# Moves of small steps to GpSimd, exits of v's products in one copy, no comparison for empty rows, and a fifth pair in four-step products

## The chip, the cores and the metric

The kernel runs on one core of a Trainium2 chip. The metric is the device time of one execution in microseconds. Three runs of the kernel before took 1397.51, 1401.68 and 1403.38 us; their median, 1401.68 us, is the time before. The core has five engines that work side by side, each in the order of its own instructions: TensorE (PE; its weight loads are listed as PEld), VectorE (DVE), ScalarE (ACT), GpSimd (POOL) and the queue that issues transfers (SP). They wait for each other by semaphores.

## The reference

Attention of 8 batches with 8 heads over 576 tokens with 64 features, in which a score counts only if it is within tau of its row's maximum, and then two layers of an MLP (4608 tokens, 512 to 2048 to 512) with a leaky step between them:

```python
scores = scale * np.matmul(q, k.transpose(0, 1, 3, 2))
thresh = np.max(scores, axis=-1, keepdims=True) - tau
scores = np.where(scores >= thresh, scores, -1000000000.0)
scores = scores - np.max(scores, axis=-1, keepdims=True)
attn = np.exp(scores)
attn = attn / (np.sum(attn, axis=-1, keepdims=True) + 1e-09)
x = np.matmul(attn, v)            # then heads side by side: 4608 x 512
h = x @ w_in
g = np.maximum(h, 0.0) + alpha * np.minimum(h, 0.0)
out = (g @ w_out).astype(np.float32)
```

The weights w_in and w_out arrive as float64 and are read as pairs of 32-bit words; the kernel makes two float32 parts (high and low) of each.

## The kernel before

**Pairs, units, cycles.** Two heads of one batch make a pair; there are 32. A pair has nine units of 128 rows of queries (`UNITS`): four chunks for each head and one tail that holds the last 64 rows of both. The program runs in cycles, one unit per cycle, nine cycles a pair, from cycle -3 to 291. In cycle i the mask of unit i is applied, the scores of unit i + 2 are computed, and maximum and exp of unit i + 2 follow (before cycle `SW` = 52 these come in twos: in an odd cycle i the maximum and exp of unit i + 1 at its start and of unit i + 2 at its end). The chain of a unit is: `scores` on TensorE into one of two PSUM buffers `s` (L395); `rowmax` on DVE, the negated maximum `nmx` (L410); `expo` on ACT, `p` (L418), and then the threshold `thr` = maximum - tau (L423, ACT); `mask` on DVE (L430), which compares the scores with `thr`, multiplies `p` and sums the row into `sm`, and with which the buffer `s` is free again; `turn` on TensorE (L439, L455), which transposes `p`.

**Whole and split pairs.** The transposed `p` is copied out of PSUM for the product with v. In the first `WHOLE` = 4 pairs it is copied whole, as float32 (L499, three copies in four on ACT and one on DVE), and the product (L542, `avmul`) runs in TensorE's slower float32 form with 64 columns of v, one matmul per block. In the other 28 pairs it is split into a high part (`hi`, L491, ACT) and a low part (`lo`, L495, DVE), v likewise (`prep_vh` L370 on ACT, `prep_vl` L375 on POOL), with high and low part of v as 64 + 64 columns of one operand `vst`; two matmuls per block. The product of a split pair leaves PSUM in `avout` in two copies on ACT, of 64 partitions each: the high half into `xa` (L553) and the low half into `xb` (L555).

**The end of a pair.** `recip` adds 1e-9 to the sums and inverts them (L560, L561, DVE); `rturn` and `rout` bring the result by way of DRAM into `rb`, spread over 64 partitions; `fin_add` (POOL) adds `xb` to `xa` for a split pair (L582, L586) and takes the mean of v into `vs` (L583); `fin_mul` multiplies with `rb` (L589, POOL); `fin_un` (L592, DVE) compares `rb` with 1e8 to find rows that kept no score and puts `vs` there; `fin_out` adds that (L595, POOL) and writes `xs` (L596, SP). The cycles for these, counted from the pair's first, are in `FINW` (whole) and `FINS` (split).

**Beside it.** q and k of later pairs are loaded, split and doubled ten or more cycles ahead: `prep_kl` (L332) and `prep_ql` (L357) on POOL, the scaling of q by 0.125 on ACT (L345 into `qst`, L350 in place), and moves between partitions on SP (L337 to L364). Seven pieces of w_in and seven of w_out are decoded in cycles -3 to 40, a new piece every three cycles (`Split64`): `size` on ACT, `clamp` (L127), `shift` (L130), `sign` (L135) and `power` (L140) on DVE, `round` on ACT, `rest` (L148, L149) and `join` (L152) on POOL. Which of DVE and POOL takes clamp and the two products of `rest` is in `ENG1`, letters v and p. From cycle 49 on `Mlp` puts layer 1 and 2 for 7 of the 16 blocks of w_in beside attention (`pha`, `acca`, `ga`); how much goes into a cycle is planned by counts, not by time. What is left follows in `drain`, with the decoding of the other weights, and then the other nine blocks (`phb`, `accb`).

**What sets the order.** On PE, ACT, DVE and POOL the instructions stand in the order in which the program names them, cycle by cycle; `at_cycle` puts a step into a cycle. The order in SP's queue is set by a scheduler. An engine that waits holds up everything behind it.

## Time and profile before

| | |
|---|---|
| median of three runs | 1401.68 us |
| span of the profiled execution | 1397.3 us |
| busy TensorE, DVE, ACT, POOL | 1339.4, 975.7, 820.9, 762.3 us |
| instructions on DVE, ACT, POOL | 1933, 1843, 821 |
| bytes moved by DMA | 157.67 MB, 113 GB/s in the mean |
| granted clock of TensorE | 0.9 or more of full speed in every one of 40 slices |

Attention takes the first 823 us or so (the last mask stands at 820.80 us), the drain goes on to about 950 us, and the rest is the second part of the MLP. A row of a table of stages reads: start and end of the stage, its length, and for each engine the busy time and, in brackets, the number of instructions; then the granted clock, the share of time in which the DMA engines were busy, and GB/s. A row of groups reads: line, engine, operation, tiles written and read, shapes, count; busy time in us and the mean of one in ns; idle time of the engine just before them and who ended it. A row of a timeline: start and duration in us, engine, line, operation. A row of waits: who waited for whom, us in total, times, the longest.

### The profile page before, as it was taken

How to read it: one execution, taken by the hardware profiler on the slowest of the kernel's cores; microseconds unless marked ns; L12 is line 12 of the kernel's file. 1: busy time of each engine (PE TensorE's matmuls, PEld its weight loads, DVE VectorE, ACT ScalarE, POOL GpSimd, SP SyncE). 2: the span in 40 equal slices, each digit the busy share in tenths (PEclk: the TensorE clock that was granted, in tenths of full speed). 3: DMA queues.
4: the chain of work that ended last, by engine and by line, in shares of the span. 5: the costliest groups of instructions: out<-in, count | busy, mean ns of one | idle time of the engine just before them, and what ended most of it. 6: DMA issues, size and time to landing. Idle time of an engine off the chain costs nothing.

```text
span 1397.3 us, 23301 instructions
## 1 busy us (share of the span) xinstructions
PE 1339.4 (96%) x8116; PEld 1181.2 (85%) x8116; DVE 975.7 (70%) x1933; ACT 820.9 (59%) x1843; POOL 762.3 (55%) x821
## 2 busy tenths in 40 slices
PE   5888899999999999999999999888999999999998
PEld 4556789999999999999999998777888888888887
DVE  6999988888888898898888957986323323323332
ACT  7788888888888888888888854453112012111100
POOL 3776676666676666576676557566434124223311
PEclk9999999999999999999999999999999999999999
DMA  8643634545545444454454214433320220111011
GB/s 249 184 127 106 180 105 122 162 116 142 147 117 150 139 134 131 132 154 127 128 160 132 83 57 153 132 109 128 121 74 17 91 91 33 59 61 42 19 61 38
DMA packets 94628, 157.67 MB, mean 113 GB/s; under 512 B 14160, under 2 KB 39024, under 8 KB 94512
## 3 DMA queue, kind: packets, MB, share of 16 engines
q1 hardware_dynamic: 94512, 156.19, 38.4%
q8 instruction: 65, 1.06, 0.3%
q14 instruction: 51, 0.42, 0.1%
HBM read 85.53 MB, written 28.46 MB: 82 GB/s over the span
## 4 chain that ended last, share of the span: by engine, by line
PE 80%; DVE 9%; ACT 4%; DMA 2%; issue 2%; POOL 2%; SPq 0%; DVEq 0%; POOLq 0%; ACTq 0%
PE phb L194 16%; PE accb L224 16%; PE s L395 10%; PE av L542 10%; PE acca L224 9%; PE pha L194 9%; PE t L439 7%; DVE p L430 2%; DVE nmx L410 2%; DMA wri<-in_moe_w_in_dram 1%; PE tk L455 1%; DVE wti L135 1%; POOL wi L152 1%; ACT xb L555 1%; ACT xa L553 1%
## 5 line engine op out<-in xcount | busy, mean ns | idle before, releaser
L410 DVE TENSOR_REDUCE nmx<-s 128x1 f32<-128x576 f32 x288 | 217.0, 753 | 72.6 <-PE s L395 69.5
L215 ACT ACTIVATE gb<-ptb 128x512 fp32r<-128x512 f32 x81 | 50.9, 630 | 337.7 <-DVE ptb L873 337.3
L218 POOL TENSOR_TENSOR gb<-ptb,gb 128x512 fp32r<-128x512 f32 x81 | 104.4, 1290 | 257.0 <-ACT gb L215 256.8
L224 PE MATMUL acca<-wo,ga 128*128 128x512 f32 x756 | 230.7, 419 | 7.2 <-ACT ga L215 4.0
L224 PE MATMUL accb<-wo,gb 128*128 128x512 f32 x972 | 221.9, 389 | 0.0
L224 PEld LDWEIGHTS accb<-wo,gb 128*128 128x128 f32 x972 | 182.4, 188 | 37.9
L430 DVE SCALAR_TENSOR_TENSOR p<-s,thr,p 128x576 f32<-128x576 f32 x256 | 206.6, 807 | 1.3 <-ACT thr L423 0.9
L194 PE MATMUL phb<-xh,wi 128*128 128x512 f32 x648 | 202.9, 392 | 1.1 <-ACT xh L180 1.1
L194 PE MATMUL pha<-xh,wi 128*128 128x256 f32 x1008 | 199.7, 284 | 3.7 <-DVE pta L873 3.4
L418 ACT ACTIVATE p<-s,nmx 128x576 f32<-128x576 f32 x256 | 190.0, 742 | 10.8 <-DVE nmx L410 10.5
L395 PE MATMUL s<-kh,qst 128*128 128x288 f32 x640 | 142.2, 312 | 38.1 <-DVE p L430 23.3
L194 PEld LDWEIGHTS pha<-xh,wi 128*128 128x128 f32 x1008 | 163.8, 190 | 9.9 <-DVE pta L873 4.6
L224 PEld LDWEIGHTS acca<-wo,ga 128*128 128x128 f32 x756 | 132.8, 191 | 28.6 <-ACT ga L215 5.3
L439 PE MATMUL t<-ident,p 128*128 128x128 f32 x1024 | 154.6, 274 | 0.0
L395 PEld LDWEIGHTS s<-kh,qst 128*128 128x128 f32 x640 | 101.4, 193 | 61.5 <-issue 29.4
L903 DVE TENSOR_TENSOR ob<-accb,pin 128x512 f32<-128x512 f32 x36 | 24.2, 689 | 181.9 <-PE accb L224 181.9
L194 PEld LDWEIGHTS phb<-xh,wi 128*128 128x128 f32 x648 | 122.6, 189 | 27.2 <-ACT xh L180 1.5
L194 PE MATMUL pha<-xl,wi 128*128 128x256 f32 x504 | 142.2, 282 | 0.0
L872 DVE TENSOR_SCALAR ptb<-phb,alpha_sb 128x512 f32<-128x512 f32 x81 | 60.7, 751 | 108.5 <-PE phb L194 96.4
L395 PE MATMUL s<-kl,qst 128*128 128x288 f32 x640 | 133.8, 299 | 0.0
L194 PE MATMUL phb<-xl,wi 128*128 128x512 f32 x324 | 127.2, 393 | 3.6 <-POOL xl L182 3.6
L439 PEld LDWEIGHTS t<-ident,p 128*128 128x128 f32 x1024 | 126.5, 141 | 0.1
(117 smaller groups left out, 2772.6 us busy)
## 6 DMA issues: line engine op xcount, KB each, us to landing
kr<-in_k_dram SPq DMA_DIRECT2D x31, 320.0 KB
rb<-rvd SPq DMA_DIRECT2D x64, 144.0 KB
...
```

The source lines that it names most:

```text
L194: nc.tensor.matmul(ph[:, :n], w[:, c, :], xx[:, c, :n], start=(c == 0 and ti == 0), stop=(c == NCC - 1 and ti == 2),)
L215: nc.scalar.activation(g[:, 0, :n], t[:, :n], AF.Copy)
L218: nc.gpsimd.tensor_tensor(g[:, 1, :n], t[:, :n], f(g[:, 0, :n]), op=ALU.subtract)
L224: nc.tensor.matmul(acc[:m, :], gg[:, g, o : o + m], w, start=(first and ti == 0), stop=(last and ti == 2))
L395: nc.tensor.matmul(ps[:, h, :288], w, kk[:, a + h * 288 : a + (h + 1) * 288], start=(ki == 0 and i == 0), stop=(ki == 1 and i == n - 1),)
L410: nc.vector.tensor_reduce(self.nmx[:, j : j + 1], self.S[u][0][:, :, :288], axis=AX.XY, op=ALU.max, negate=True)
L418: nc.scalar.activation(pj, ps[:, :, :288], AF.Exp, bias=nmx[:, j : j + 1], scale=1.0)
L430: nc.vector.scalar_tensor_tensor(pj, ps[:, :, :288], thr[:, j : j + 1], pj, op0=ALU.is_ge, op1=ALU.mult, accum_out=self.sm[:, c : c + 1])
L439: nc.tensor.transpose(tb[:, c, :], pt[:, j, j * D + c * P : j * D + (c + 1) * P], ident)
L542: nc.tensor.matmul(pa[:m, :n], w, x, start=(part == 0 and c == 0), stop=(part == z.parts[-1] and c == NKC))
L872: nc.vector.tensor_scalar(t[:, :n], ph[:, :n], 0.0, alpha_sb[:, fc : fc + 1], op0=ALU.min, op1=ALU.mult)
L903: nc.vector.tensor_tensor(ob[:m], acc[:m], pi_[:m], op=ALU.add)
```

## The change

- `clamp` of all 14 early pieces goes from DVE to POOL (`ENG1`), with minimum and maximum in the other order; `shift` comes a cycle later, just ahead of `sign`.
- The threshold of units before cycle 50 (`THRP`) is computed on POOL instead of ACT. The scaling of q in place (L350) goes from ACT to POOL, the addition before the reciprocal from DVE to POOL.
- A fifth pair, pair 4, is whole (`WHOLE`); the memory of the whole pairs and the decoding is given to the MLP in cycle 49 instead of 41 (`SPC`).
- For split pairs the second head's v has its low part in the first 64 columns and its high part in the others. `avout` copies all 128 partitions at once, of the first head into `xa` and of the second into `xb`. Three moves in SP's queue (`part_low`, `part_high`) bring the low parts together in `xl` (in the buffer of `qt`) and the high parts in `xa`. `prep_vl` becomes two instructions.
- The comparison for empty rows goes. `vs` is now 1e-9 times the mean of v and is added to the sum ahead of the multiplication with `rb`, by POOL, with one input tensor; the addition in `fin_out` goes.
- `FINW` and `FINS` move the last steps: `xs` of a split pair is written in cycle 18 of the pair instead of 16, of a whole pair in 17 as before.

```diff
-ENG1 = ('vpp', 'vpp')
+ENG1 = ('ppp', 'ppp')
-THR = 'a'
+THRP = 50
-FINW = (9, 10, 11, 14, 16, 16, 17)
-FINS = (9, 11, 12, 12, 15, 16, 16)
+FINW = (9, 10, 11, 14, 14, 15, 16)
+FINS = (9, 11, 12, 13, 14, 16, 17)
-SPC = 41
-WHOLE = 4
+SPC = 49
+WHOLE = 5
...
-            self.eng[0].tensor_scalar(f(self.t), f(self.t), WORD_LO, WORD_HI, op0=ALU.max, op1=ALU.min)
+            self.eng[0].tensor_scalar(f(self.t), f(self.t), WORD_HI, WORD_LO, op0=ALU.min, op1=ALU.max)
...
-            nc.scalar.activation(self.qr, self.qr, AF.Copy, scale=0.125)
+            nc.gpsimd.tensor_scalar(self.qr, self.qr, 0.125, None, op0=ALU.mult)
...
-            self.vst = ap1.tile([P, 10, P], F32R, tag="vst", name=f"vst{self.pi}", bufs=2)
-            nc.scalar.activation(self.vst[:, :, :D], self.vr, AF.Copy)
+            self.vst = ap1.tile([P, 11, P], F32R, tag="vst", name=f"vst{self.pi}", bufs=2)
+            at = self.vst.rearrange("p c d -> p (c d)").rearrange("p (j r) -> p j r", j=2)
+            self.vh = at[:, :, : 5 * P].rearrange("p j (c d) -> p j c d", d=P)[:, :, :, :D]
+            nc.scalar.activation(self.vh, self.vr.rearrange("p (j c) d -> p j c d", j=2), AF.Copy)
...
-            nc.gpsimd.tensor_tensor(self.vst[:, :, D:], self.vr, f(self.vst[:, :, :D]), op=ALU.subtract)
+            for j in range(2):
+                vl = self.vst[:, 5 * j : 5 * j + 5, (1 - j) * D : (2 - j) * D]
+                nc.gpsimd.tensor_tensor(vl, self.vr[:, 5 * j : 5 * j + 5], f(self.vh[:, j]), op=ALU.subtract)
...
-            if THR == "p" and 9 * self.pi + u >= SW:
+            if 9 * self.pi + u < THRP:
                 nc.gpsimd.tensor_scalar(self.S[u][2][:, c], nmx[:, c], -1.0, tau_sb, op0=ALU.mult, op1=ALU.subtract)
...
-            r, cs = slice(j * D, (j + 1) * D), slice(col, col + n)
-            nc.scalar.activation(self.xa[r, cs], pa[:D, :n], AF.Copy)
-            if not self.whole:
-                nc.scalar.activation(self.xb[r, cs], pa[D:, :n], AF.Copy)
+            if self.whole:
+                nc.scalar.activation(self.xa[j * D : (j + 1) * D, cs], pa[:D, :n], AF.Copy)
+            else:
+                nc.scalar.activation((self.xb if j else self.xa)[:, cs], pa[:, :n], AF.Copy)
+        def part_low(self):
+            if not self.whole:
+                self.xl = ap1.tile([P, S + 4], F32, tag="qt", name=f"xl{self.pi}", bufs=1)
+                nc.sync.dma_start(self.xl[:D, 2:], self.xa[D:, 2:])
+                nc.sync.dma_start(self.xl[D:, : S + 2], self.xb[:D, : S + 2])
+        def part_high(self):
+            if not self.whole:
+                nc.sync.dma_start(self.xa[D:, : S + 2], self.xb[D:, : S + 2])
...
-            nc.vector.tensor_scalar(self.rv, self.sm, 1e-9, None, op0=ALU.add)
+            nc.gpsimd.tensor_scalar(self.rv, self.sm, 1e-9, None, op0=ALU.add)
             nc.vector.reciprocal(self.rv, self.rv)
...
-                nc.gpsimd.tensor_scalar(self.vs[r], xa[r, cs], 1.0 / S, None, op0=ALU.mult)
+                nc.gpsimd.tensor_scalar(self.vs[r], xa[r, cs], 1e-9 / S, None, op0=ALU.mult)
...
+        def fin_un(self):
+            nc.gpsimd.tensor_scalar(self.x, self.x, self.vs, None, op0=ALU.add)
         def fin_mul(self):
             nc.gpsimd.tensor_tensor(self.x, self.x, self.rb, op=ALU.mult)
-        def fin_un(self):
-            nc.vector.tensor_scalar(self.rb, self.rb, 1e8, self.vs, op0=ALU.is_ge, op1=ALU.mult)
         def fin_out(self):
-            nc.gpsimd.tensor_tensor(self.x, self.x, self.rb, op=ALU.add)
             nc.sync.dma_start(xs[self.b][self.hp], self.x)
...
-        at_cycle(o + fin[3], p.fin_add)
-        at_cycle(o + fin[4], p.fin_mul)
+        at_cycle(o + fin[3], p.part_low)
+        at_cycle(o + fin[4], p.part_high)
+        at_cycle(o + fin[5], p.fin_add)
         at_cycle(o + fin[5], p.fin_un)
-        at_cycle(o + fin[6], p.fin_out)
+        at_cycle(o + fin[6], p.fin_mul)
+        at_cycle(o + fin[6] + 1, p.fin_out)
...
-        at_cycle(c + 2, w.shift)
+        at_cycle(c + 3, w.shift)
```

Three places in the order of the instructions follow. In a row stand the line, the operation, the tile written and the tiles read, and the size; the lines of the changed kernel are its own (L426 is the threshold, L579 the addition before the reciprocal, L609 `fin_un`, L612 the product with `rb`).

POOL in cycles 24 to 26, near the end of pair 2 (`vs`, `xa` or `x` and `rb` belong to pair 1, `kl` to pair 3, `wro`, `wto`, `wo` to pieces of w_out). Before:

```order
L583 TENSOR_SCALAR vs_963<-xa_729 64x1 x2
L148 TENSOR_TENSOR wro_746<-wro_746 128x512
L149 TENSOR_TENSOR wto_845<-wto_845,wo_973 128x512
L589 TENSOR_TENSOR xa_729<-xa_729,rb_878 128x576
L332 TENSOR_TENSOR kl_1028<-kr_970,kh_1026 128x640
L152 TENSOR_TENSOR wo_973<-wto_845,wro_746 128x512
L595 TENSOR_TENSOR xa_729<-xa_729,rb_878 128x576
```

After:

```order
L603 TENSOR_SCALAR vs_992<-x_729 64x1 x2
L609 TENSOR_SCALAR x_729<-x_729,vs_992 128x576
L148 TENSOR_TENSOR wro_746<-wro_746 128x512
L149 TENSOR_TENSOR wto_844<-wto_844,wo_969 128x512
L426 TENSOR_SCALAR thr_7_973<-nmx_7_972,tau_sb 128x1
L612 TENSOR_TENSOR x_729<-x_729,rb_877 128x576
L332 TENSOR_TENSOR kl_1026<-kr_966,kh_1024 128x640
L152 TENSOR_TENSOR wo_969<-wto_844,wro_746 128x512
L426 TENSOR_SCALAR thr_0_1038<-nmx_0_1037,tau_sb 128x1
L127 TENSOR_SCALAR wto_1031<-wto_1031 128x512
L426 TENSOR_SCALAR thr_0_1038<-nmx_0_1037,tau_sb 128x1
```

The steps that were there stand in the same order; thresholds now stand between them, a clamp stands at the end, and the last addition (L595) has become `fin_un` (L609) ahead of the product.

DVE in cycles 25 to 27, where pair 3 begins (`s_7`, `s_8` are the last units of pair 2, `s_0`, `s_1` the first of pair 3). Before:

```order
L430 SCALAR_TENSOR_TENSOR p_3_979,sm_715<-s_7_950,thr_7_977,p_3_979 128x576
L410 TENSOR_REDUCE nmx_7_976<-s_8_983 128x1
L592 TENSOR_SCALAR rb_878<-rb_878,vs_963 128x576
L135 SCALAR_TENSOR_TENSOR wto_940<-wro_848,wto_940 128x512
L410 TENSOR_REDUCE nmx_0_1038<-s_0_1005 128x1
L430 SCALAR_TENSOR_TENSOR p_3_979,sm_715<-s_8_983,thr_7_977,p_3_979 128x576
L140 TENSOR_SCALAR wro_848<-wto_940 128x512
L127 TENSOR_SCALAR wto_1032<-wto_1032 128x512
L430 SCALAR_TENSOR_TENSOR p_0_1041,sm_1004<-s_0_1005,thr_0_1039,p_0_1041 128x576
L410 TENSOR_REDUCE nmx_0_1038<-s_1_1045 128x1
L560 TENSOR_SCALAR rv_1092<-sm_715 128x9
L561 RECIPROCAL rv_1092<-rv_1092 128x9
```

After:

```order
L435 SCALAR_TENSOR_TENSOR p_3_975,sm_716<-s_7_949,thr_7_973,p_3_975 128x576
L415 TENSOR_REDUCE nmx_7_972<-s_8_979 128x1
L130 TENSOR_SCALAR wto_939<-wto_939 128x512
L135 SCALAR_TENSOR_TENSOR wto_939<-wro_847,wto_939 128x512
L415 TENSOR_REDUCE nmx_0_1037<-s_0_1004 128x1
L435 SCALAR_TENSOR_TENSOR p_3_975,sm_716<-s_8_979,thr_7_973,p_3_975 128x576
L140 TENSOR_SCALAR wro_847<-wto_939 128x512
L435 SCALAR_TENSOR_TENSOR p_0_1040,sm_1003<-s_0_1004,thr_0_1038,p_0_1040 128x576
L415 TENSOR_REDUCE nmx_0_1037<-s_1_1044 128x1
L580 RECIPROCAL rv_1090<-rv_1090 128x9
```

Comparison (L592), clamp (L127) and addition (L560) are gone; shift (L130) and sign (L135) stand side by side, and the reciprocal, alone, reads what POOL's L579 writes.

SP's queue after the load of the next k, at a split pair in the middle of attention (`rvd` and `rb` carry the reciprocals, `part` takes results of the MLP). Before:

```order
L364 DMA qst_110<-qt_6333 64x576
L305 DMA kr_6497<-in_k_dram 128x640
L709 DMA part_81<-po_128_6362 128x512
L570 DMA rvd_163<-rt_6412 9x128
L574 DMA rb_6415<-rvd_163 64x576 x2
```

After:

```order
L364 DMA qst_110<-qt_6281 64x576
L305 DMA kr_6442<-in_k_dram 128x640
L569 DMA xl_6398<-x_6095 64x578
L589 DMA rvd_163<-rt_6358 9x128
L570 DMA xl_6398<-x_6139 64x578
L574 DMA x_6095<-x_6139 64x578
L593 DMA rb_6361<-rvd_163 64x576 x2
```

Three moves of 64 partitions stand between the load of k and the spread of the reciprocals: the two low parts into `xl`, and then the high part of the second head into the `x` of the first.

More of the change, by code (lines that the diff above doesn't have):

```diff
@@ L539, in avmul @@
                 for c in cs:
-                    w = self.vst[:, j * NKC + c if c < NKC else 8 + j, :]
+                    w = self.vst[:, 5 * j + c, :]
                     x = rhs[part][:, c, :] if c < NKC else tr[part]
@@ L546, in avout @@
         def avout(self, step, j):
-            if (step, j) == (0, 0):
-                self.xa = ap1.tile([P, S + 4], F32, tag="xa", name=f"xa{self.pi}", bufs=2)
-                if not self.whole:
-                    self.xb = ap1.tile([P, S + 4], F32, tag="xb", name=f"xb{self.pi}", bufs=1)
             pa, col, n = self.av.pop((step, j))
-            r, cs = slice(j * D, (j + 1) * D), slice(col, col + n)
-            nc.scalar.activation(self.xa[r, cs], pa[:D, :n], AF.Copy)
-            if not self.whole:
-                nc.scalar.activation(self.xb[r, cs], pa[D:, :n], AF.Copy)
+            cs = slice(col, col + n)
+            if step == 0 and (j == 0 or not self.whole):
+                x = ap1.tile([P, S + 4], F32, tag="xb" if j else "xa", name=f"x{j}{self.pi}", bufs=2 - j)
+                if j == 0:
+                    self.xa = x
+                else:
+                    self.xb = x
+            if self.whole:
+                nc.scalar.activation(self.xa[j * D : (j + 1) * D, cs], pa[:D, :n], AF.Copy)
+            else:
+                nc.scalar.activation((self.xb if j else self.xa)[:, cs], pa[:, :n], AF.Copy)
+        def part_low(self):
+            if not self.whole:
+                self.xl = ap1.tile([P, S + 4], F32, tag="qt", name=f"xl{self.pi}", bufs=1)
[4 more added lines that the diff above has]
+                nc.sync.dma_start(self.xa[D:, : S + 2], self.xb[D:, : S + 2])
         def recip(self):
             self.rv = ap1.tile([P, 9], F32, tag="rv", name=f"rv{self.pi}", bufs=2)
-            nc.vector.tensor_scalar(self.rv, self.sm, 1e-9, None, op0=ALU.add)
+            nc.gpsimd.tensor_scalar(self.rv, self.sm, 1e-9, None, op0=ALU.add)
             nc.vector.reciprocal(self.rv, self.rv)
```

10 lines of the change are left out of this document (5 added, 5 removed).

## The prediction

> **What bounds the kernel now.** I read first the busy time of each engine by stage, with cuts where pairs of heads begin: pair 0, pairs 1 to 3, pair 4 with four cycles of pair 5, the start of the MLP, the long middle, the drain.
>
> ```profile
> core 0: us, PE busy (x) PEld busy (x) DVE busy (x) ACT busy (x) POOL busy (x), PEclk, DMA share, GB/s
> 14.50:36.86 22.36, 18.41 (x91) 14.71 (x92) 20.94 (x42) 19.67 (x44) 12.58 (x10) 1.00 0.82 253
> 36.86:116.91 80.05, 69.79 (x378) 45.66 (x376) 76.81 (x138) 66.10 (x151) 58.00 (x49) 1.00 0.52 147
> 116.91:151.14 34.23, 27.36 (x177) 21.89 (x176) 31.33 (x68) 27.47 (x64) 16.69 (x15) 1.00 0.55 149
> 151.14:200.00 48.86, 43.67 (x323) 41.71 (x322) 43.79 (x99) 42.76 (x102) 35.53 (x43) 0.97 0.51 142
> 200.00:800.00 600.00, 598.75 (x4372) 570.50 (x4371) 528.70 (x1174) 515.30 (x1230) 391.43 (x494) 1.00 0.48 134
> 800.00:1000.00 200.00, 185.21 (x1042) 159.26 (x1041) 142.75 (x235) 87.03 (x167) 125.94 (x108) 0.97 0.37 119
> ```
>
> Two regimes stand here. From 200 to 800 us TensorE is busy for 598.75 of 600 us: what is taken from DVE, ACT or GpSimd there shortens nothing. Before 151 us DVE is the full engine: 76.81 of 80.05 us (96%) in pairs 1 to 3, against 58.00 for POOL (72%) and 66.10 for ACT (83%). The waits between 14.5 and 151 us say which way the dependence goes:
>
> ```profile
> PE s L395 <- DVE p L430: 18.5, 19, 2.3
> ```
>
> TensorE's scores wait 18.5 us in all for the mask (L430), which frees their buffer. So a gain must come out of the first 150 us. Behind them the plan gives the MLP its work by cycle number, so a head start is carried through the full middle to the end.
>
> **What leaves DVE.** The time of single lines of code on DVE in pairs 1 to 3, in this order: the clamp L127, the shift L130, the sign L135, the power L140, the addition before the reciprocal L560, the comparison for empty rows L592.
>
> ```profile
> 36.86:116.91 80.05, 8.47 (x10) 1.00 0.52 147
> 36.86:116.91 80.05, 8.79 (x10) 1.00 0.52 147
> 36.86:116.91 80.05, 9.53 (x10) 1.00 0.52 147
> 36.86:116.91 80.05, 6.09 (x10) 1.00 0.52 147
> 36.86:116.91 80.05, 2.42 (x3) 1.00 0.52 147
> 36.86:116.91 80.05, 1.52 (x3) 1.00 0.52 147
> ```
>
> L127, L560 and L592 leave: 8.47 + 2.42 + 1.52 = 12.4 us. But those that stay do not stay as they are. The timeline of DVE, and one row of POOL's:
>
> ```profile
> 12.41 0.43 DVE L127 TENSOR_SCALAR wti<-wti 128x512 f32<-128x512 f32 x1
> ...
> 69.82 0.41 DVE L140 TENSOR_SCALAR wri<-wti 128x512 int32<-128x512 int32 x1
> 70.16 0.68 DVE L135 SCALAR_TENSOR_TENSOR wto<-wro,wto 128x512 int32<-128x512 int32 x1
> ...
> 73.19 1.52 DVE L127 TENSOR_SCALAR wto<-wto 128x512 f32<-128x512 f32 x1
> ```
> ```profile
> 73.06 1.36 POOL L152 TENSOR_TENSOR wi<-wti,wri 128x512 fp32r<-128x512 f32 x1
> ```
>
> The same clamp takes 0.43 us at 12.41 and 1.52 us at 73.19, where it cannot finish before POOL's L152 is done at 74.42. Free of POOL, L130 (as L140, the same shape), L135 and L140 cost 0.41 + 0.68 + 0.41 = 1.5 us a piece of weights, 15 for ten pieces; the rows sum to 24.4. So 9.4 us are waits for POOL, met while POOL is busy 72% of the time. If POOL rises to 95% I scale them to 12.4: 3.0 us come back. DVE then wants 76.81 - 12.4 + 3.0 = 67.4 us; at its present 96%, 70.2 instead of 80.05.
>
> The Trainium skill ("SBUF — State Buffer", Who interferes with whom) states this as an exclusive lock on a pair of ports that VectorE and GpSimd share; the 1.52 against 0.43 us agree. "Perfetto Trace Analysis" of the Trainium skill (Optimizing Scalar/DVE Operations) draws from it that offloading between those two "might not help": that is rival 2.
>
> **What POOL takes on.** Groups of POOL in the same stage, and one of the whole run:
>
> ```profile
> L149 POOL TENSOR_TENSOR wto<-wto,wo 128x512 f32<-128x512 f32 x5 | 6.4, 1273 | 1.2 <-ACT wo L144 1.2
> ...
> L148 POOL TENSOR_TENSOR wro<-wro 128x512 f32<-128x512 f32 x5 | 5.7, 1131 | 2.4 <-issue 1.4 <-DVE wro L140 1.0
> L332 POOL TENSOR_TENSOR kl<-kr,kh 128x640 fp32r<-128x640 f32 x3 | 4.9, 1631 | 5.8 <-ACT kh L328 4.1 <-PE t L439 1.7
> ...
> L589 POOL TENSOR_TENSOR xa<-xa,rb 128x576 f32<-128x576 f32 x3 | 4.4, 1475 | 0.0
> L595 POOL TENSOR_TENSOR xa<-xa,rb 128x576 f32<-128x576 f32 x3 | 4.2, 1398 | 0.0
> L375 POOL TENSOR_TENSOR vst<-vr,vst 128x640 fp32r<-128x640 f32 x1 | 1.6, 1558 | 0.2 <-POOL vs L583 0.2
> L583 POOL TENSOR_SCALAR vs<-xa 64x1 f32<-64x1 f32 x6 | 1.2, 205 | 7.4 <-ACT xa L553 6.3 <-DVE wto L135 0.9
> ```
> ```profile
> L217 POOL CAST ga<-pta 128x256 fp32r<-128x256 f32 x95 | 37.7, 397 | 3.3
> ```
>
> No one-input operation of 512 or 576 columns is on POOL in the trace. Below it lies the cast of 256 columns (0.40 us), above it the two-input L148 of 512 (1.13). A line through 205 ns for one column and 397 for 256 gives an estimate of 0.59 us for 512 and 0.64 for 576. I take that line, since cast and scalar operation are the nearest in kind, and keep 1.13 as the other end. The Trainium skill ("GPSIMD Engine Reference", Engine selection) calls one-input work "roughly line-rate"; at the 1.2 GHz that the page gives, an estimate of 0.43 us for 512. No row here shows it; ten clamps would then cost 1.6 us less than in my sum.
>
> Added in pairs 1 to 3: 27 thresholds at 0.21 (5.6), ten clamps at 0.59 (5.9), three scalings of q at 0.64 (1.9), three additions at 0.2 (0.6). Cheaper or gone: the last addition L595 (1.40) becomes a one-input one of 0.64, three times (-2.3), and v's low part for pair 4 (L375, -1.6). POOL: 58.0 + 10.1 = 68.1 us of work. Small instructions do not follow each other without a gap:
>
> ```profile
> 828.47 0.73 POOL L211 TENSOR_TENSOR pta<-pta,pra 128x256 f32<-128x256 f32 x1
> 829.26 0.40 POOL L217 CAST ga<-pta 128x256 fp32r<-128x256 f32 x1
> ```
>
> From 829.20 to 829.26 are 0.06 us; at 0.08 with some 42 new instructions, 71.5. At 1.13 us for every one-input operation it would be 80, the whole stage.
>
> So both engines want 70 to 72 of these 80 us, and they are tied together nine times a pair: POOL's threshold waits for DVE's maximum and everything behind it in POOL's queue with it; DVE's mask waits for the threshold, and the scores after next wait for that mask. Once a pair DVE's reciprocal now also waits for POOL's addition. Bounds for the stage: -10 if the two overlap freely, +12 by rival 3. I take 76.5, **-3.5**, which fills POOL to 94%, nearly what DVE reaches now.
>
> **The other stages.** Pair 0: three clamps of 0.42 leave a DVE that is 94% full, POOL stands at 56%: **-1**. Pair 4 loses its low parts. Two sums over the run, of the subtractions L495 (28 split pairs) and the copies L499 (four whole pairs):
>
> ```profile
> sum 785.50, DVE 198.97; mean DVE 39.79
> ```
> ```profile
> sum 785.50, DVE 6.21 ACT 20.16; mean DVE 1.24 ACT 4.03
> ```
>
> 7.1 us for a split pair on DVE, 1.6 for a whole one: -5.5, with two additions and a comparison -6.3. 31.33 becomes 25.0; at the present 92% that is 27 us instead of 34.2. But the chain of one buffer of scores stays (scores, maximum, exp, threshold, mask, two buffers in turn), and TensorE alone is busy for 27.36 us of this stage. I take 30, **-4**; bounds -7 and -1. Pair 4's products cost TensorE no more:
>
> ```profile
> L542 PE MATMUL av<-eo,vst 128*128 128x322 f32 x448 | 86.8, 317 | 0.0
> ...
> L542 PE MATMUL av<-eo,vst 128*64 128x322 f32 x64 | 20.8, 447 | 0.0
> ```
>
> 0.33 us each, but 8 where 16 of 0.19 stood. From 151 to 200 us ACT loses the scaling of q and half of the exits, DVE some 1 us a pair: **-0.5**, bounds -2 and 0. From 200 to 800 us: **0**, bounds -3 and +3. There the three new moves a pair in SP's queue, and well under 1 us a pair more on POOL (65% busy), lie beside TensorE; what they delay (the next k and q, loaded ten or more cycles ahead) is not due. The thresholds that leave ACT before cycle 50 gain nothing of themselves, since ACT is not the full engine. The later shift, the order of minimum and maximum, and the later opening of the MLP's memory (no earlier user) I cost at nothing.
>
> **The end of attention.** The last pair's output gates the drain. Its exit on ACT, its moves in SP's queue, and a row of the chain that ended last:
>
> ```profile
> 831.13 0.43 ACT L555 ACTIVATE xb<-av 64x322 f32<-64x322 f32 x1
> ```
> ```profile
> 831.88 0.29 SPq L570 DMA_DIRECT2D rvd<-rt  x1
> 833.24 1.09 SPq L574 DMA_DIRECT2D rb<-rvd  x2
> ...
> 840.13 0.32 SPq L596 DMA_DIRECT2D xs<-xa  x1
> ```
> ```profile
> 841.64 5.87 DMA xr<-xs
> ```
>
> After the exit at 831.6 two moves now follow each other, at about 2 us each (rvd to rb took 1.4 to the next issue), then 2.3 us of sums, 0.64 and 1.2: about 841 instead of 840.1. **+1**, bounds 0 and 3.
>
> **The sum** stands against the profiled execution, whose span is 1397.3 us: -1 - 3.5 - 4 - 0.5 + 0 + 1 = -8. The runs shown lie from 1397.51 to 1403.38, so that execution was among the short ones; I carry the difference to the median 1401.68: **1393.7**.
>
> **Rivals.** (1) DVE alone counts and POOL is never late: pairs 1 to 3 at 70.2 (-9.8), pair 4 at 27 (-7), the rest as above: -17, 1384.4. For it: 12.4 us really leave the fullest engine. Against it: POOL has almost no slack left. (2) POOL gives back in waits and lateness all that DVE saves in pairs 1 to 3, and pair 4 stays: -4.5, 1397.2. For it: 71.5 us of demand on POOL against 67.4 on DVE, in program order. (3) Slower: thresholds stand in line behind POOL's blocks. In the new order the product with rb, L332 and L152 come between two thresholds (1.48 + 1.63 + 1.36 = 4.5 us), and before that the scaled sums, L148 and L149 (0.41 + 0.64 + 1.13 + 1.27 = 3.5). If both fall wholly into DVE's path, a pair pays 8 us against 4.1 saved: +12 over three pairs, less 5.5 in the other stages, +1 at the end: +7.5, 1409. It decides once masks come more than 2 us late twice a pair. Against it: a threshold is queued one to two masks ahead, and its maximum is done by then.
>
> **Chances.** Forecast 0.45, rival 1 0.15, rival 2 0.27, rival 3 0.13. About 0.5% (7 us) is what a measurement of this kernel can tell from no change. Of the forecast's own spread (-12 to -3) some 0.27 lies beyond -7; with rival 1 and a little of rival 2, faster is 0.44. Slower by as much is the larger part of rival 3: 0.10. The same: 0.46. The range 1385 to 1406 leaves out half of rival 1 and most of rival 3.
>
> **What would show it.** Right: cycle 48 ends near 143 us instead of 151; in pairs 1 to 3 POOL is over 90% busy and DVE under 90%; the mask has a new wait for POOL's threshold, in sum under 1 us a pair; the middle is still full on TensorE. Wrong: one-input operations of 512 columns near 1.1 us on POOL; mask waits of several us a pair; gaps on TensorE after 200 us; a drain whose first load comes more than 3 us later than the head start allows.

## The result, and the profile after

| | time, us (median, range) | runs | ratio to before, 95% interval |
|---|---|---|---|
| before | 1401.35 (1397.51 to 1403.38) | 4 | |
| changed | 1422.45 (1421.95 to 1424.99) | 4 | 1.0162 (1.0144 to 1.018) |

The changed kernel is slower by 1.6%, outside the predicted range. The spans of the two profiled executions are 1397.3 and 1420.2 us, 22.9 us apart, and the question is where these lie. The masks (L435, one per cycle) mark the same points of the program in both traces, so I cut the table of stages of the changed kernel there: pair 0, pairs 1 to 3, pair 4 with four cycles of pair 5, up to pair 8, up to pair 31, from the last mask to the write of the last `xs`, and the rest.

```profile
core 0: us, PE busy (x) PEld busy (x) DVE busy (x) ACT busy (x) POOL busy (x), PEclk, DMA share, GB/s
14.71:42.17 27.46, 21.44 (x97) 16.36 (x97) 19.42 (x38) 17.43 (x34) 19.06 (x23) 0.81 0.66 205
42.17:131.21 89.04, 71.38 (x372) 45.91 (x370) 64.44 (x123) 58.50 (x119) 78.95 (x90) 0.98 0.46 132
131.21:164.92 33.71, 31.01 (x168) 20.48 (x168) 24.86 (x51) 22.09 (x46) 24.59 (x33) 1.00 0.50 139
164.92:232.40 67.48, 60.83 (x452) 57.98 (x452) 56.21 (x125) 49.34 (x122) 49.29 (x61) 0.97 0.50 134
232.40:815.90 583.50, 582.50 (x4241) 552.44 (x4240) 496.25 (x1092) 441.58 (x1079) 436.81 (x549) 1.00 0.57 153
836.96:858.90 21.94, 21.65 (x143) 19.70 (x141) 5.89 (x14) 6.47 (x15) 14.24 (x21) 1.00 0.24 72
858.90:1420.20 561.30, 538.34 (x2487) 446.88 (x2485) 243.06 (x355) 118.97 (x187) 222.58 (x152) 0.99 0.24 76
```

The same table of the kernel before, for the stages that the prediction did not cut this way:

```profile
151.14:216.30 65.16, 59.97 (x446) 57.29 (x445) 58.02 (x129) 56.17 (x137) 46.84 (x59) 0.97 0.43 120
216.30:799.00 582.70, 581.46 (x4240) 553.92 (x4240) 513.46 (x1138) 500.89 (x1194) 379.19 (x478) 1.00 0.49 136
820.80:840.13 19.33, 19.11 (x126) 17.32 (x125) 5.65 (x15) 6.41 (x16) 11.40 (x17) 1.00 0.18 59
840.13:1397.30 557.17, 538.91 (x2502) 447.72 (x2500) 244.92 (x357) 120.33 (x188) 222.66 (x152) 0.99 0.24 77
```

The lengths differ by +5.1 (pair 0), +9.0 (pairs 1 to 3), -0.5, +2.3, +0.8 (the middle), +2.6 (the end of attention) and +4.1 us (behind it); pair 31 up to its last mask gives -0.7. So 14 of the 22.9 us are lost in the first four pairs. There DVE is not the full engine any more: 64.44 of 89.04 us (72%, before 96%), and POOL is, with 78.95 (89%, before 72%). The waits between 14.5 and 132 us (who waited for whom, us in total, times, longest):

```profile
PE s L400 <- DVE p L435: 16.6, 12, 2.6
DVE p L435 <- POOL thr L426: 14.4, 10, 3.0
DVE rv L580 <- POOL rv L579: 4.9, 3, 2.8
```

TensorE still waits for the mask, as before. The mask's wait for the threshold on POOL is new, 14.4 us in ten times. One place shows how it arises, the one whose order is printed with the change (POOL in cycles 24 to 26): POOL's timeline, then DVE's masks.

```profile
91.20 0.49 POOL L603 TENSOR_SCALAR vs<-x 64x1 f32<-64x1 f32 x2
91.81 1.74 POOL L609 TENSOR_SCALAR x<-x,vs 128x576 f32<-128x576 f32 x1
93.51 1.21 POOL L148 TENSOR_TENSOR wro<-wro 128x512 f32<-128x512 f32 x1
94.68 1.73 POOL L149 TENSOR_TENSOR wto<-wto,wo 128x512 f32<-128x512 f32 x1
96.51 0.30 POOL L426 TENSOR_SCALAR thr<-nmx,tau_sb 128x1 f32<-128x1 f32 x1
96.79 1.20 POOL L612 TENSOR_TENSOR x<-x,rb 128x576 f32<-128x576 f32 x1
97.95 1.72 POOL L332 TENSOR_TENSOR kl<-kr,kh 128x640 fp32r<-128x640 f32 x1
99.64 1.27 POOL L152 TENSOR_TENSOR wo<-wto,wro 128x512 fp32r<-128x512 f32 x1
100.90 0.29 POOL L426 TENSOR_SCALAR thr<-nmx,tau_sb 128x1 f32<-128x1 f32 x1
```
```profile
96.85 0.82 DVE L435 SCALAR_TENSOR_TENSOR p<-s,thr,p 128x576 f32<-128x576 f32 x1 [0.92 <-POOL thr L426]
101.22 0.82 DVE L435 SCALAR_TENSOR_TENSOR p<-s,thr,p 128x576 f32<-128x576 f32 x1 [2.95 <-POOL thr L426]
```

The threshold at 96.51 stands behind 5.2 us of POOL's work, the one at 100.90 behind another 4.1. Each mask begins right when its threshold is done, after 0.92 and 2.95 us in which DVE did nothing.

Pair 0 has one thing more, the granted clock of 0.81 in its row. The trace puts it into one stretch, shown here with the matching one of before:

```profile
26.34:36.58 10.24, 8.72 (x29) 6.38 (x30) 8.02 (x15) 4.03 (x9) 8.26 (x9) 0.50 0.28 71
```
```profile
26.00:36.86 10.86, 9.62 (x53) 6.56 (x54) 10.31 (x22) 9.62 (x24) 5.50 (x5) 1.00 0.55 149
```

In 10.24 us at a granted clock of 0.50 TensorE did 29 matmuls; before, it did 53 in 10.86 us at 1.00. The stretch begins at the end of a wait of 3.7 us (before: 1.3 us) of TensorE for the mask of the tail unit, which itself had waited 1.8 us for its threshold on POOL. That the low clock came of the late mask and made its loss larger is argued: the clock was not varied by itself, and its share of the 5.1 us is not measured.

Four kinds of one-input operations on POOL in the whole run (count, busy us, mean ns, idle before them):

```profile
L609 POOL TENSOR_SCALAR x<-x,vs 128x576 f32<-128x576 f32 x32 | 55.6, 1737 | 3.3
L350 POOL TENSOR_SCALAR qr<-qr 128x576 f32<-128x576 f32 x31 | 52.0, 1679 | 18.2 <-ACT qst L345 16.4 <-DMA kh<-kh 1.3
L426 POOL TENSOR_SCALAR thr<-nmx,tau_sb 128x1 f32<-128x1 f32 x50 | 16.6, 331 | 16.3 <-DVE nmx L415 14.8 <-DMA kr<-in_k_dram 0.3
L127 POOL TENSOR_SCALAR wto<-wto 128x512 f32<-128x512 f32 x7 | 4.3, 613 | 0.6
```

The clamp takes 0.61 us, as estimated (0.59). The scaling of q and the addition of the mean take 1.68 and 1.74 us where the prediction had 0.64. So two things are suspected: the queue of thresholds, and operations 2.6 times as long as thought.

### The profile page after: what moved, and what is told of

The parts are those of the page before. It is cut to its first block, busy times and chain, and to the rows that moved or that the text cites. A ratio compares the mean times of both kernels' runs of the same rounds, so it can differ in the third digit from the quotient of the medians.

```text
span 1420.2 us, 23308 instructions
## 1 busy us (share of the span) xinstructions
PE 1350.9 (95%) x8116; PEld 1182.0 (83%) x8116; DVE 933.3 (66%) x1841; ACT 736.4 (52%) x1647; POOL 860.6 (61%) x971
## 4 chain that ended last, share of the span: by engine, by line
PE 77%; POOL 8%; DVE 6%; DMA 4%; issue 3%; ACT 1%; SPq 0%; POOLq 0%; DVEq 0%; ACTq 0%
PE accb L224 16%; PE phb L194 15%; PE av L547 11%; PE s L400 10%; PE pha L194 9%; PE acca L224 9%; PE t L444 7%; DMA wro<-in_moe_w_out_dram 1%; DMA wri<-in_moe_w_in_dram 1%; DVE wto L135 1%; PE tk L460 1%; POOL qr L350 1%; POOL wto L149 1%; DVE p L435 1%; POOL ga L218 1%
## 5 line engine op out<-in xcount | busy, mean ns | idle before, releaser
L218 POOL TENSOR_TENSOR gb<-ptb,gb 128x512 fp32r<-128x512 f32 x81 | 104.4, 1291 | 259.5 <-ACT gb L215 259.5
L224 PE MATMUL accb<-wo,gb 128*128 128x512 f32 x972 | 221.9, 390 | 0.0
L435 DVE SCALAR_TENSOR_TENSOR p<-s,thr,p 128x576 f32<-128x576 f32 x256 | 207.0, 808 | 22.4 <-POOL thr L426 18.5
L924 DVE TENSOR_TENSOR ob<-accb,pin 128x512 f32<-128x512 f32 x36 | 24.1, 689 | 179.0 <-PE accb L224 179.0
```

Source lines behind the costliest of these rows:

```text
L218: nc.gpsimd.tensor_tensor(g[:, 1, :n], t[:, :n], f(g[:, 0, :n]), op=ALU.subtract)
L224: nc.tensor.matmul(acc[:m, :], gg[:, g, o : o + m], w, start=(first and ti == 0), stop=(last and ti == 2))
L435: nc.vector.scalar_tensor_tensor(pj, ps[:, :, :288], thr[:, j : j + 1], pj, op0=ALU.is_ge, op1=ALU.mult, accum_out=self.sm[:, c : c + 1])
L924: nc.vector.tensor_tensor(ob[:m], acc[:m], pi_[:m], op=ALU.add)
```

## The experiments

In these, "before" was run again beside each kernel; its medians were 1399.75 to 1400.68 us, against 1401.35 beside the changed kernel. So a difference of two medians that stood beside different runs of before is uncertain by up to 1.6 us; each ratio is taken against the before that ran beside it. Where a stage is compared, one profile of each kernel is used. Three kernels with the same early steps (a4, d1, g1) took 77.3, 77.3 and 77.4 us for pairs 1 to 3, but 63.2, 66.6 and 64.5 us from cycle 49 to pair 8.

| run | median, us | ratio to before, 95% interval |
|---|---|---|
| a1: thresholds on ACT | 1416.39 | 1.0113 (1.0094 to 1.0132) |
| a2: clamps on DVE | 1422.74 | 1.0166 (1.0143 to 1.0189) |
| a3: scaling on ACT, addition on DVE | 1407.32 | 1.0053 (1.0033 to 1.0073) |
| a4: all of these | 1398.32 | 0.9986 (0.9974 to 0.9997) |
| b1: before, fifth whole pair | 1401.83 | 1.0013 (1.0001 to 1.0024) |
| b2: before, thresholds on POOL | 1408.22 | 1.0058 (1.0039 to 1.0076) |
| d1: a4, last pair's exits in two copies | 1399.92 | 0.9998 (0.9986 to 1.001) |
| e1: a4, clamps on POOL | 1403.23 | 1.0032 (1.0018 to 1.0047) |
| f1: changed, two-operation form | 1406.03 | 1.0042 (1.003 to 1.0053) |
| f2: f1, thresholds on ACT, addition on DVE | 1401.00 | 1.0007 (0.9991 to 1.0023) |
| g1: d1, two-operation form | 1395.83 | 0.9978 (0.9966 to 0.999) |

### Each group back by itself (a1, a2, a3), and all together (a4)

```diff
-THRP = 50
+THRP = 0
```

> The changed kernel with the thresholds back on ACT (THRP = 0); clamps, scaling of q and the addition before the reciprocal stay on GpSimd. Theory Q (thresholds queue behind GpSimd's blocks, and the mask behind them): the waits of the mask for the threshold (14.4 + 1.8 us in pairs 0 to 3) go, pair 8 starts at 232.4 - 13 = about 219 us, and the time falls from 1422 to about 1408. Theory D (GpSimd simply has too much work there: 79.0 of 89.1 us busy in pairs 1 to 3, of which the thresholds are some 10): only their own time comes back, pair 8 starts at about 226, time about 1416. Under both the 6.7 us that the time behind the last mask grew stay.

Measured: 6.1 us less than the changed kernel, and pair 8 starts at 221.9 us instead of 232.4. The time is the one that D expected, the start of pair 8 nearer to that of Q: neither has the whole of it.

```diff
-ENG1 = ('ppp', 'ppp')
+ENG1 = ('vpp', 'vpp')
-        at_cycle(c + 3, w.shift)
+        at_cycle(c + 2, w.shift)
```

> The changed kernel with the early clamps (and the shift's cycle) back on DVE; thresholds stay on GpSimd. Theory D: GpSimd loses 13 clamps of 0.61 us (8 us) in pairs 0 to 3 and pair 8 starts about 6 us earlier, near 226; time about 1416. Theory Q: the thresholds still stand behind the blocks of 3.5 and 4.5 us, so little changes: pair 8 between 230 and 234, time 1420 to 1424.

Measured: the same time as the changed kernel, pair 8 at 230.1 us. Eight us of work taken off POOL bring nothing as long as the rest stands, as theory Q had it. Theory D is not ruled out by this run alone, since the clamps load DVE in exchange: in pairs 1 to 3 it is busy for 72.27 us instead of 64.44.

```diff
-            nc.gpsimd.tensor_scalar(self.qr, self.qr, 0.125, None, op0=ALU.mult)
+            nc.scalar.activation(self.qr, self.qr, AF.Copy, scale=0.125)
...
-            nc.gpsimd.tensor_scalar(self.rv, self.sm, 1e-9, None, op0=ALU.add)
+            nc.vector.tensor_scalar(self.rv, self.sm, 1e-9, None, op0=ALU.add)
```

> The changed kernel with the scaling of q (L350, 1.82 us each on GpSimd) back on ACT and the addition before the reciprocal back on DVE. Theory Q: thresholds still queue, but behind blocks shorter by 1.8 us once a pair: pair 8 about 4 us earlier (228), time about 1418. Theory D: GpSimd loses 7.3 + 0.8 us in pairs 0 to 3, pair 8 near 225 to 227, time about 1415. If neither the scaling nor the addition matters, pair 8 stays at 232.

Measured: 15.1 us less, twice what D expected and more than three times what Q did. Pair 8 starts at 223.8, and from there to pair 31 the kernel needs 577.4 us instead of 583.5: a part that I had not thought of lies in the middle.

> All three groups back (thresholds and scaling on ACT, clamps and the addition on DVE); what stays of the change is the fifth whole pair, the exits in one copy with three moves, and the way without a comparison. Both theories: the early loss goes, pair 8 starts at 216.3 less about 4 for the fifth whole pair, 212; the time is then 1397.3 - 4 plus what the time behind the last mask grew (6.7 us, if it comes from the exits): about 1400. If the early loss comes from the fifth pair or the exits instead, pair 8 stays above 220 and the time above 1410.

Measured: 1398.32. Pair 8 starts at 210.1 us, so the early loss is gone and what remains of the change gains 6 us there. From pair 8 to pair 31 it takes 577.5 us against 582.7 of before. Behind the last mask it gives back 11 us (587.6 against 576.5). The three groups together are the whole loss, and more than the sum of their parts: 6.1 + 15.1 - 0.3 = 20.9 of 24.1 us.

### One-input operations by themselves (m1)

```diff
+        cases = [
+            ("mnmx", lambda a: e.tensor_scalar(a, a, WORD_HI, WORD_LO, op0=ALU.min, op1=ALU.max)),
+            ("mul", lambda a: e.tensor_scalar(a, a, 0.125, None, op0=ALU.mult)),
+            ("mx", lambda a: e.tensor_scalar(a, a, 0.125, None, op0=ALU.max)),
+            ("muladd", lambda a: e.tensor_scalar(a, a, 0.125, 1.0, op0=ALU.mult, op1=ALU.add)),
+            ("addcol", lambda a: e.tensor_scalar(a, a, col, None, op0=ALU.add)),
...
```

> Only a measurement: the attention and the MLP are left out (the output is zeros). One-input operations on GpSimd, in place, 512 and 576 columns, twice each, first with VectorE idle and then (576) beside a row of shifts on VectorE: min and max (as the clamp), times 0.125 (as the scaling of q), plus a constant, max alone, times and plus, plus one number per partition (as fin_un), times one number per partition. Theory 'form': operations that multiply or add take 3 ns a column whatever VectorE does, min and max 1.2 ns: 576 columns about 1.75 us against 0.69. Theory 'lock': all forms take 1.2 ns a column when VectorE is idle (0.61 for 512, 0.69 for 576), and the 1.74 to 1.82 us of L350 and L609 are waits for VectorE, which show in the busy row only. Theory 'width': 576 columns cost more than 512 for every form.

Groups of POOL with VectorE idle, and two of those beside a row of shifts on VectorE (`busy`):

```profile
L106 POOL TENSOR_SCALAR addcol<-addcol,col 128x576 f32<-128x576 f32 x2 | 3.4, 1724 | 0.1
L102 POOL TENSOR_SCALAR mul<-mul 128x576 f32<-128x576 f32 x2 | 3.3, 1648 | 0.2
L104 POOL TENSOR_SCALAR mx<-mx 128x576 f32<-128x576 f32 x2 | 3.3, 1647 | 0.1
L105 POOL TENSOR_SCALAR muladd<-muladd 128x576 f32<-128x576 f32 x2 | 1.3, 672 | 0.1
L101 POOL TENSOR_SCALAR mnmx<-mnmx 128x576 f32<-128x576 f32 x2 | 1.3, 666 | 0.2
...
L102 POOL TENSOR_SCALAR mulbusy<-mulbusy 128x576 f32<-128x576 f32 x2 | 4.0, 1978 | 0.1
L101 POOL TENSOR_SCALAR mnmxbusy<-mnmxbusy 128x576 f32<-128x576 f32 x2 | 1.4, 724 | 0.2
```

None of the three theories has it whole. The kind of operation does not matter: a maximum alone takes 1.65 us, times and plus together 0.67. What matters is whether the instruction carries one operation or two. With one it takes 2.5 times as long, with VectorE idle; in the last two rows, a busy VectorE adds 0.33 and 0.06 us. Theory 'width' fails too: with 512 columns one constant operation took 1.77 to 1.89 us, more than with 576, and no run here says why. The clamp has two operations, the scaling and the addition of the mean have one.

### The same steps in the other form (f1), and then the thresholds too (f2)

```diff
-            nc.gpsimd.tensor_scalar(self.qr, self.qr, 0.125, None, op0=ALU.mult)
+            nc.gpsimd.tensor_scalar(self.qr, self.qr, 0.125, 1.0, op0=ALU.mult, op1=ALU.mult)
...
-            nc.gpsimd.tensor_scalar(self.x, self.x, self.vs, None, op0=ALU.add)
+            nc.gpsimd.tensor_scalar(self.x, self.x, self.vs, 1.0, op0=ALU.add, op1=ALU.mult)
```

> The changed kernel; only the scaling of q (L350) and the addition of the mean (L609) get a second operation that changes nothing (times 1.0), so that they take the form that measured 0.67 us for 576 columns instead of 1.65 to 1.72. Same engine, same place, same operands. Theory 'form' (a one-operation tensor_scalar is what was mis-sized, and that is the larger part of the loss): both take about 0.7 us, GpSimd loses about 1.1 us times seven in pairs 0 to 3, the products with v no longer wait in the middle (pairs of 25.2 instead of 25.5 us), and the time falls by 12 to 15 us, to 1408 to 1411, as with both steps off GpSimd. Theory 'place' (it is the wait for ACT's copy of q and the queue behind it that cost, not the duration): the time stays above 1416.

The two groups of POOL in this kernel:

```profile
L609 POOL TENSOR_SCALAR x<-x,vs 128x576 f32<-128x576 f32 x32 | 24.0, 750 | 3.3
L350 POOL TENSOR_SCALAR qr<-qr 128x576 f32<-128x576 f32 x31 | 21.3, 688 | 32.9 <-ACT qst L345 32.7
```

Measured: 1406.03, 16.4 us less than the changed kernel, with every step on the same engine and in the same place. The two profiles are 14.4 us apart. Theory 'form' is right about the size, but not about the place: pairs 1 to 3 take 88.77 us instead of 89.04 and pair 0 is 1.7 us shorter; 3.4 us lie in pairs 4 to 7, 6.2 between pair 8 and pair 31 (577.3 us), and 2.7 behind the last mask.

In pairs 1 to 3 the mask's waits for the threshold fall from 14.2 to 4.2 us, and yet the stage is as long: POOL's threshold now waits 9.3 us for DVE's maximum instead of 5.0, and the granted clock is 0.94 instead of 0.98, with TensorE busy for 73.82 us instead of 71.38. So the long form by itself does not account for the loss there.

In the middle it does. From 300 to 800 us this is the wait of DVE's L206, a step of the MLP, for POOL (changed, then this run):

```profile
DVE pta L206 <- POOL ga L218: 10.7, 17, 0.9
```
```profile
DVE pta L206 <- POOL ga L218: 0.3, 1, 0.3
```

It happens 17 times in some 20 pairs. In the changed kernel, for example, L350 runs on POOL from 412.39 to 414.05 us. Behind it L218 ends at 415.22, DVE's L206 begins at 415.26, ACT's L207 behind that ends at 416.16, and TensorE's product with v (L547), which by the trace waits for L207, begins at 416.21. Over the 500 us the matmuls around these products start 5.2 us further apart in sum than in this run. Their ends are modelled, so that the stage has a busy share of 99.8% (582.50 of 583.50) although TensorE stands still for a moment once a pair.

```diff
-THRP = 50
+THRP = 0
...
-            nc.gpsimd.tensor_scalar(self.rv, self.sm, 1e-9, None, op0=ALU.add)
+            nc.vector.tensor_scalar(self.rv, self.sm, 1e-9, None, op0=ALU.add)
```

> As the run before, and the thresholds are back on ACT and the addition before the reciprocal on DVE; clamps and the scaling of q stay on GpSimd. If the queue of thresholds and the form are the whole loss, this equals the kernel with only the clamps on GpSimd (1403.2) or is 1 to 3 us better, since ACT loses the scaling and the two-operation addition saves 1 us a pair: 1400 to 1403. If it is above 1406, the scaling costs by its place too.

Measured: 1401.00, as expected: another 5.0 us, and no difference from before that can be told. The equality has two parts, though: pair 8 starts at 220.4 us, 4.1 later than before, and the middle is 5.1 us shorter (577.6 against 582.7). And against e1 below, from which it differs only in the engine of the scaling and the form of L609, pairs 1 to 3 take 85.1 us instead of 80.9. So the scaling on POOL still costs there when it is short. Part of that can be the granted clock (0.94 against 0.98).

### The thresholds alone, on a POOL with room (b2)

```diff
-            if THR == "p" and 9 * self.pi + u >= SW:
+            if 9 * self.pi + u < 50:
```

> The kernel before, with only the thresholds of units 0 to 49 on GpSimd. Theory Q (the mask waits behind GpSimd's blocks, even when GpSimd has 28% to spare): the mask has waits for the threshold of 8 us or more before 151 us, pair 8 starts at 222 to 226 instead of 216, time 1406 to 1409. Theory D (thresholds cost only once GpSimd is nearly full): waits under 3 us, time within 2 us of 1400.

Measured: 1408.22, 8.4 us more than before; pairs 1 to 3 take 85.9 us instead of 80.05, and pair 8 starts at 223.1. The time and the start are those of theory Q, but the sign that I had named is not there: the mask's waits for the threshold sum to 3.2 us between 14.5 and 132 us, not 8. The timeline of POOL and of DVE at the end of pair 3 shows what happens instead:

```profile
112.76 0.39 POOL L421 TENSOR_SCALAR thr<-nmx,tau_sb 128x1 f32<-128x1 f32 x1 [2.13 <-DVE nmx L410]
113.12 1.03 POOL L148 TENSOR_TENSOR wro<-wro 128x512 f32<-128x512 f32 x1
114.12 1.27 POOL L149 TENSOR_TENSOR wto<-wto,wo 128x512 f32<-128x512 f32 x1
115.38 0.28 POOL L421 TENSOR_SCALAR thr<-nmx,tau_sb 128x1 f32<-128x1 f32 x1
115.64 1.20 POOL L589 TENSOR_TENSOR xa<-xa,rb 128x576 f32<-128x576 f32 x1
```
```profile
113.62 0.81 DVE L430 SCALAR_TENSOR_TENSOR p<-s,thr,p 128x576 f32<-128x576 f32 x1
...
116.87 1.78 DVE L592 TENSOR_SCALAR rb<-rb,vs 128x576 f32<-128x576 f32 x1 [2.43 <-POOL xa L589]
118.57 1.76 DVE L135 SCALAR_TENSOR_TENSOR wto<-wro,wto 128x512 int32<-128x512 int32 x1
```

POOL's threshold waits 2.13 us for DVE's maximum (20.4 us in all before 132 us), and all of POOL's queue with it. Then the product L589 comes late, DVE's comparison waits 2.43 us for it, and DVE's next mask, at 120.26 us, stands behind that and behind two operations of 1.78 and 1.76 us (the comparison took 0.51 each in the mean before). The thresholds tie two queues together in both directions, and that POOL had 28% of pairs 1 to 3 to spare before did not help.

### The clamps alone (e1)

```diff
-ENG1 = ('vpp', 'vpp')
+ENG1 = ('ppp', 'ppp')
-        at_cycle(c + 2, w.shift)
+        at_cycle(c + 3, w.shift)
```

> The changed kernel with thresholds and scaling back on ACT and the addition back on DVE; only the clamps stay on GpSimd. If DVE alone sets the pace of pairs 1 to 3 when GpSimd has room, the 7 to 8 us of clamps that leave it show as 5 us or more: pair 4 starts at 109 us or earlier (114.4 with the clamps on DVE), time about 1393. If GpSimd's share (the lock and its queue) takes it back, pair 4 starts between 113 and 116 and the time stays at 1398.

Both expectations failed: it is 4.9 us slower than a4, and pair 4 starts at 120.5 us. Pairs 1 to 3 of e1, and of a4:

```profile
39.60:120.50 80.90, 71.28 (x377) 46.79 (x377) 69.14 (x126) 64.72 (x148) 63.12 (x59) 0.98 0.51 145
```
```profile
37.10:114.40 77.30, 69.99 (x377) 45.70 (x376) 72.86 (x136) 65.16 (x150) 58.82 (x49) 1.00 0.56 156
```

DVE loses 3.7 us and ten instructions, and the stage grows by 3.6. The ten clamps took 8.3 us in a4; sign and power take 4.0 of it back (L135 11.95 us instead of 8.79, L140 6.43 instead of 5.55). A DVE at 94% was thus not the limit in the sense in which the sum used it. The trace of e1 has waits that a4's has less of (POOL's clamp for ACT's words, 1.7 us at 52 us; the maximum for the scores, 8.1 us before 70 us against 2.8); which of them is the first cause stays open. The Trainium skill ("Perfetto Trace Analysis", Optimizing Scalar/DVE Operations) warns that offloading from VectorE to GpSimd "might not help"; this run agrees, with 1403.23 against 1398.32 us.

### The fifth pair alone (b1)

```diff
-SPC = 41
-WHOLE = 4
+SPC = 49
+WHOLE = 5
```

> The kernel before with the fifth whole pair and the later opening of the MLP's memory alone (WHOLE = 5, SPC = 49). If the fifth pair brings what the kernel with all three groups back shows (pair 8 at 210.1 instead of 216.3), pair 8 starts 4 to 5 us earlier, near 212, and the middle keeps its 582.7 us. If the drain's growth (11 us in that kernel behind the last mask) comes from the exits, the rest stays at 576.5 and the time is about 1397; if it comes from the fifth pair or the later memory, the rest is near 587 and the time 1405 or more.

The expectation failed. Pair 4 takes 22.6 us instead of 24.4, but pair 5 then 28.8 instead of 23.6, and pair 8 starts at 218.9, later than before. The middle (582.6) and the time behind the last mask (577.8) are close to those of before (582.7 and 576.5), so neither the gain in the middle nor the loss behind it comes from this part. Why pair 5 is longer was not tried apart; in a4 it takes 24.7.

### The end of attention (d1)

```diff
+            elif last:
+                nc.scalar.activation(self.xa[r, cs], pa[r, :n], AF.Copy)
+                nc.scalar.activation(self.xl[r, cs], pa[(1 - j) * D : (2 - j) * D, :n], AF.Copy)
...
-            if not self.whole:
+            if not self.whole and self.pi < npairs - 1:
                 nc.sync.dma_start(self.xa[D:, : S + 2], self.xb[D:, : S + 2])
```

> The kernel with all three groups back, and the last pair's exits in two copies per product straight to their partitions, without the three moves. Theory M (the moves on the last pair's path gate the drain): xs is written about 18.5 to 19.5 us after the last mask instead of 22.4, and the 3 to 4 us are gained in the end; time about 1394. Theory S (the drain's own order, which a scheduler sets, is what costs the other 8 us): the rest behind xs stays at 565 or moves by more than the 3 us either way. If neither, the time stays at 1398.

The write of `xs` in a4, where the last mask stands at 808.61 us, and in d1 (there L622), where it stands at 813.88:

```profile
830.96 0.32 SPq L615 DMA_DIRECT2D xs<-x  x1
```
```profile
832.82 0.33 SPq L622 DMA_DIRECT2D xs<-x  x1
```

From the last mask to `xs` it is 22.4 us with the moves and 18.9 without, as theory M had named it, and the time behind the last mask falls by 4.1 (587.6 to 583.5). But this counts from a point that has itself moved: up to its last mask pair 31 takes 23.3 us here (and in g1), in a4 21.05. From the start of pair 31 (787.56 in a4, 790.55 here) to `xs` it is 43.4 us with the moves and 42.3 without, so they are worth 1.1 us on this path, one profile each. The median shows no gain (1399.92); in the profiled run pairs 5 to 7 took 3.4 us longer than in a4, although the steps there are the same, which one profile each cannot place. What lies behind `xs` stays at 564.6 us, 7 more than before. The drain's instructions are ordered by a scheduler, and DVE, ACT and POOL have them in another order in the changed kernel than before. Two slices of the drain of the changed kernel, and one of before:

```profile
959.00:979.00 20.00, 15.20 (x56) 11.71 (x54) 12.71 (x18) 6.90 (x12) 10.51 (x7) 0.83 0.36 120
979.00:999.00 20.00, 15.39 (x56) 12.34 (x57) 16.06 (x20) 7.38 (x10) 13.40 (x8) 0.83 0.42 140
```
```profile
940.00:960.00 20.00, 14.94 (x54) 11.04 (x53) 16.94 (x22) 8.35 (x14) 13.84 (x8) 0.83 0.34 111
```

Before, TensorE has one such hole where the second part of the MLP begins, of 3.6 us; now it has two, of 4.0 and 5.4 us, each with a granted clock of 0.83. The other runs bear out that this goes with the order. In a1 to a4 and e1 the drain stands in the order of the changed kernel or very nearly so: there are two holes, of 3.5 to 4.1 and 5.2 to 7.1 us, and 562.0 to 565.2 us behind `xs` (561.3 in the changed kernel, 557.2 before). In f1 and f2 it stands nearly in the order of before: one hole of 3.6 us, and 559.9 and 558.2 us. The second operation in L350 and L609 was enough to turn the order. It was not changed with everything else held, so what it costs in us is not shown.

### What remains of the change, in its best form (g1)

a4 with the edits of d1, and with the addition of the mean in two operations.

> What stays of the change when all that went to GpSimd is back where it was: fifth whole pair, exits in one copy except for the last pair (two copies straight to their partitions), no comparison, and the addition of the mean in the two-operation form. If the gains measured apart add up (1.4 us of the kernel with all groups back, up to 4 us behind the last mask, about 1 us a pair of GpSimd before 151 us): 1394 to 1397. If the drain's order or the early stage takes it back as in the run with the last pair's exits: 1398 to 1400.

Measured: 1395.83 us in nine runs, faster than before by 0.22% (0.1 to 0.34) and 26.6 us below the changed kernel. That is the first case of the expectation. Against d1, which differs in the form of L609 alone, it is 4.1 us; but the drain has another order again, and of the 4.0 us between the two profiles 2.6 lie behind the last mask.

## Why the prediction was wrong

The step that failed is the stage of pairs 1 to 3: "I take 76.5, -3.5". It took 89.04 us, +9.0. The sum let DVE's saved time shorten the stage, and set aside the thresholds on POOL with the argument that "a threshold is queued one to two masks ahead, and its maximum is done by then". In its place the runs show that every group of steps that goes to POOL lengthens this stage: the thresholds alone by 5.9 us (b2 against before), the clamps alone by 3.6 (e1 against a4), a short scaling of q by another 4.2 (f2 against e1). For the thresholds the traces show how, by tying the queues of DVE and POOL together; for clamps and scaling the first cause stays open. With all three groups back it is 77.3 us (a4). A second step failed apart from it: the middle at 0, where POOL's part was to "lie beside TensorE" and the scaling in its long form cost 6.2 us (f1).

The runs, undone step by step, make up the difference: 1422.45 (changed), 1406.03 (form of L350 and L609, -16.4), 1401.00 (thresholds and addition back, -5.0), 1395.83 (clamps and scaling off POOL, last pair's exits, -5.2). Counted against the before that ran beside each, they are +21.1, +6.3, +1.2 and -4.0. The order of undoing matters, since the parts work through one queue: thresholds alone are worth 6.1 taken from the changed kernel and 8.4 added to the kernel before.

- **"What POOL takes on".** This failed in size: 0.64 us for 576 columns, with 1.13 for every one-input operation as the other end. L350 takes 1.68 and L609 1.74, beyond that end. The row of the cast was not of the same form, and the two-input row was no upper bound. For the clamp, which has two operations, the line was right (0.61 against 0.59). But this is not what pairs 1 to 3 lost by: with both steps short (f1) they are 0.3 us shorter. The Trainium skill ("GPSIMD Engine Reference", Engine selection) calls one-input work "roughly line-rate". Against the estimate of 0.43 us for 512 columns that the prediction took from it, two operations measured 0.69 us and one 1.77 (m1); the measurement decides.
- **Rival 3, the threshold behind POOL's blocks.** Its mechanism is seen in pairs 0 to 3, and I gave it 0.13. Its blocks were foreseen as 3.5 and 4.5 us and measured 5.2 and 4.1. Its condition (masks late by over 2 us twice a pair) was not met: of the mask's nine waits in pairs 1 to 3, 14.2 us in all, two are over 2 us (2.95 and 2.45); the several us a pair that the prediction named as a sign of being wrong are there, 4.7. The stage lost 9.0 us all the same, and in b2 and f1 it is long with 2.8 and 4.2 us of such waits. So the mask's wait is only one half of the tie. The other half is the one that the argument left out: POOL itself waits for the maximum (14.8 us in all), and its whole queue with it.
- **"DVE then wants 67.4".** It was busy for 64.44 us, so the saving was real. That it shortens the stage was the mistake. The bounds of -10 and +12 held; the choice within them did not.
- **Pair 0, -1.** It became +5.1, with a POOL that goes from 12.58 to 19.06 us. It is 22.5 us long again in a1 and 23.9 in a3, so thresholds and scaling on POOL together cost most of it. What was not in the sum at all is the granted clock: TensorE waited 3.7 us for the tail's mask, and from the end of that wait 10.24 us stood at 0.50. In f1 and e1 it waited 3.5 and 4.0 us there, and some 6.8 us stood at 0.50; in before, a3, a4 and b2 it waited 1.1 to 1.4 us, and the clock stayed at 1.00.
- **Pair 4, -4.** It became -0.5, and b1 shows that the fifth pair alone gives nothing by pair 8.
- **The middle, 0.** The total is right (+0.8) by luck, from two parts that I had not seen: the one-operation form of the scaling costs 6 us, and what remains of the change gains 5. It is the scaling's form and not that of L609, which is still long in a3 and a4 (577.4 and 577.5 us). Since b1 has the middle of before, the gain lies with the exits in one copy, the way without a comparison or the later last steps; these were not tried apart.
- **End of attention, +1, bounds 0 and 3.** It is +2.6 from the last mask, and +1.9 from the start of pair 31, within the bounds. The terms of the sum make 839.7 us, not 841, so the +1 did not come out of them. The moves are shown for 1.1 us of it (d1). The 4.1 us behind it were not in the sum: that the scheduler would order the drain anew was not thought of.
